# Weights in four tiles, and the first group's output product moved ahead of the third chunk pair

## The chip, the cores and the metric

The kernel runs on one core of a Trainium2 chip. The metric is device time in microseconds (us), the median of several runs. One core has a matrix engine (TensorE; PE in the profile, its weight loads are PEld), a vector engine (VectorE, DVE), a scalar engine (ScalarE, ACT), GpSimd (POOL), and a sync engine (SyncE, SP) that only issues transfers. Each takes its instructions in program order and waits on semaphores. POOL and SP issue nearly all of the DMA transfers; what POOL issues goes through the software queue (q0 in the profile), what SP issues through the hardware queue (q1).

## The reference

Two stages. First a recurrence with decay (a retention layer) over 4 batches, 8 heads, 768 steps and head size 64:

```
gamma = 1.0 - 2.0 ** (-5.0 - np.arange(H))
for t in range(S):
    state = gamma * state + k[:, :, t] (outer) v[:, :, t]
    y[:, :, t] = scale * q[:, :, t] @ state
```

Then, on the 3072 tokens of width 512 that this gives, a feed-forward layer with 2048 hidden units:

```
h = x @ w_in              # (3072, 512) @ (512, 2048)
g = h * np.cos(h)
out = g @ w_out           # (2048, 512)
```

Inputs and output are float32 in memory; the kernel multiplies in bfloat16 and accumulates in float32.

## The kernel before

**Tiles.** Time is cut into six chunks of 128 steps. A *pair* p is one chunk of two batches (b = 0, 1); there are 12 pairs, 0 to 5 for batches 0 and 1, 6 to 11 for batches 2 and 3. Two pairs are one *group* g of 512 tokens, and the feed-forward layer works by groups 0 to 5.

**Attention of one pair.** `load` brings q, k and v, 256 KB per tensor and batch ("q0" is q of batch 0). There are five sets of input buffers (`PRE`), so that pair p takes over the buffers of pair p-5. `conv_q` and `conv_v` scale q and v by powers of gamma and make bfloat16 (on DVE or POOL), `conv_k` only converts (ACT). `stage_t` transposes q and k on TensorE with the identity (L176, 16 per pair) and copies the result to `qkt` (L178 on DVE, L180 on ACT); `stage_t_dma` does the same with two DMA transposes from SP (L186). Pairs below `PT` go through TensorE. `stage_a` computes the scores (L205, 32 matmuls per pair that run two at a time), `stage_m` multiplies them by the causal mask into `am` (L214, four DVE operations per pair). `stage_y` multiplies with the running state (L228) and with v (L233), copies the result to `xt` on ACT (L237), then updates the state (L245) and copies it to `stb` (L250).

**Feed-forward.** `unit_f(g, f)` is one hidden block of 128 units for the 512 tokens of a group: four matmuls of 512 columns (L267), cosine on ACT (L258), product on DVE into `gt` (L262). `pair_f(p, r)` is the same for one pair's 256 tokens and four hidden blocks: 16 matmuls of 256 columns (L279). Its parts (0, 1) are two halves of eight matmuls. `unit_o(g, j, part)` multiplies four hidden blocks of one 128-token tile j with `w_out` (L293, four matmuls of 512 columns, 16 for a whole tile) and, after part 3, copies the bank to `ob` (ACT, L305) and stores it (SP, L306).

**PSUM.** Seven banks of 128x512 float32 are handed out from a first-in first-out list; the eighth holds the state. A matmul that takes a bank waits until the bank's last reader is done.

**Order.** It is written out by hand. After the attention of pairs 0 and 1, group 0's F blocks are computed (`pair_f` of pairs 0 and 1), with the third pair's attention (p = 2) between the last blocks; then group 1's F blocks with pair 3's attention between them; and then a regular loop over g from 1 that alternates `unit_o(g-1, ...)` with `unit_f(g, ...)` and lays one pair's attention into each half of it. Group 0's output product (64 matmuls of L293) thus comes after all of group 1's F.

**Transfers before the loop.** SP: q0, k0, q1 of pair 0; q0, v0 of pair 1; q0, q1 of pair 2; q0, q1, v0 of pair 4; then pairs 5 and 6. POOL:

```
load(nc.gpsimd, 1, ("k0", "q1", "k1", "v1"))
load_w_in(0, 256)
load_w_in(1, 256)
load_w_in(1)
...
load(nc.gpsimd, 3, ("v0", "v1"))
for r in range(4):
    load_w_out(r)
```

`w_in_sb` is one tile whose columns are in the order of memory; a load of 512 columns reads 1 MB of float32 in runs of 2 KB and writes 512 KB of bfloat16. `load_w_out(r)` reads 512 rows of 2 KB each, again 1 MB.

Of the kernel before, what the change touches and what calls it, by code (L numbers as in the profile page):

```python
# [11 lines left out]
BF16 = mybir.dt.bfloat16  # L12
# [18 lines left out]
def kernel(  # L31
# [9 lines left out]
    nc = tc.nc  # L41
# [8 lines left out]
    NP = B // 2 * NC  # L50
    NG = NP // 2
    PRE = 5
    PT = 5

    scale = 1.0 / math.sqrt(D)
    lg = [math.log(1.0 - 2.0 ** (-5.0 - h)) for h in range(H)]
# [7 lines left out]
    def sb(shape, dt, name):  # L64
        return const.tile(shape, dt, name=name)
# [8 lines left out]
    lnsc = sb([128, 1], FP32, "lnsc")  # L74
    sb([128, 1], FP32, "pad")

    w_in_sb = sb([128, KIN, DF], BF16, "w_in_sb")
    w_out_sb = sb([128, KOUT, DM], BF16, "w_out_sb")


# [24 lines left out]
    def load(eng, p, names):  # L105
        bp, c = divmod(p, NC)
        for n in names:
            t, src = SRC[n[0]]
            b = int(n[1])
            eng.dma_start(  # L110
                out=t[p % PRE][b],
                in_=src[2 * bp + b, :, ds(c * C, C)].rearrange("h t d -> t h d"))

    def load_w_in(r, n=512):
        nc.gpsimd.dma_start(
            out=w_in_sb[:, :, ts(r, n)],
            in_=moe_w_in[:, ts(r, n)].rearrange("(i p) f -> p i f", p=128))

    def load_w_out(r):
        nc.gpsimd.dma_start(  # L120
            out=w_out_sb[:, ts(r, 4), :],
            in_=moe_w_out[ts(r, 512), :].rearrange("(f p) m -> p f m", p=128))


    nc.gpsimd.iota(pos, pattern=[[C, NC]], base=1, channel_multiplier=1,
                   allow_small_or_imprecise_dtypes=True)
    load(nc.sync, 0, ("q0", "k0", "q1"))
    load(nc.sync, 1, ("q0", "v0"))
    load(nc.gpsimd, 0, ("k1", "v0", "v1"))
    make_identity(nc, ident)  # L130
    nc.vector.memset(zero, 0.0)
    nc.vector.memset(lnsc, math.log(scale))
# [17 lines left out]
    def conv_q(p, eng):  # L150
        for b in range(2):
            eng.tensor_tensor(out=qs[p % NB][:, b], in0=qf[p % PRE][b],  # L152
                              in1=bc(gq, p % NC), op=ALU.mult)

    def conv_v(p, eng):
        for b in range(2):
            eng.tensor_tensor(out=vs[p % NB][:, b], in0=vf[p % PRE][b],  # L157
                              in1=bc(gk, p % NC), op=ALU.mult)

    def conv_k(p, on_act):  # L160
        for b in range(2):
            if on_act:
                nc.scalar.copy(out=ks[p % NB][:, b], in_=kf[p % PRE][b])  # L163
            else:
                nc.vector.tensor_copy(out=ks[p % NB][:, b], in_=kf[p % PRE][b])
# [24 lines left out]
    def qt(n, b, a):  # L190
        return qkt[n][:, 0, b, a, :]

    def kt(n, b, a):
        return qkt[n][:, 1, b, a, :]

    def stage_a(p):
        n = p % NB
        todo = []
        for b in range(2):
            bk = [banks.take(), banks.take()]  # L200
            ap = [t.rearrange("p (a t) -> p a t", a=HP) for t in bk]
            for a in range(HP):
                for j in range(2):
                    po = 64 * j
                    nc.tensor.matmul(ap[j][:, a, :], lhsT=kt(n, b, a)[po : po + 64, :],  # L205
                                     rhs=qt(n, b, a)[po : po + 64, :],
                                     tile_position=(po, 0))
            todo.append((b, bk, ap))
        return todo

    def stage_m(p, item):
        b, bk, ap = item
# [51 lines left out]
    def unit_f(g, f):  # L264
        bank = banks.take()
        for i in range(KIN):
            nc.tensor.matmul(bank, lhsT=w_in_sb[:, i, ts(f, 128)], rhs=xt[g % 2][:, i, :],  # L267
                             start=(i == 0), stop=(i == KIN - 1))
        act(bank, gt[g % 2][:, f, :])
        banks.give(bank)  # L270

    def pair_f(p, r, parts=(0, 1)):

        g, hf = divmod(p, 2)
        for f in [4 * r + 2 * i for i in parts]:
            bank = banks.take()
            for e in range(2):
                for i in range(KIN):
                    nc.tensor.matmul(bank[:, ts(e, 256)], lhsT=w_in_sb[:, i, ts(f + e, 128)],  # L279
                                     rhs=xt[g % 2][:, i, ts(hf, 256)],  # L280
                                     start=(i == 0 and e == 0), stop=(i == KIN - 1),
                                     skip_group_check=True)
            act(bank, gt[g % 2][:, f : f + 2, ts(hf, 256)])
            banks.give(bank)
# [2 lines left out]

    def unit_o(g, j, part):
        if part == 0:
            o_bank[0] = banks.take()  # L290
        bank = o_bank[0]
        for f in range(4 * part, 4 * part + 4):
            nc.tensor.matmul(bank, lhsT=gt[g % 2][:, f, ts(j, 128)], rhs=w_out_sb[:, f, :],  # L293
                             start=(f == 0), stop=(f == KOUT - 1))
        if part == 3:
            o = ob[j % 4]
            bp, c = divmod(2 * g + j // 2, NC)
            dst = out[ds((2 * bp + j % 2) * S + c * C, C), :]
            if g == NG - 1 and j == 3:
                nc.vector.tensor_copy(out=o[:, ts(0, 256)], in_=bank[:, ts(0, 256)])  # L300
                nc.sync.dma_start(out=dst[:, ts(0, 256)], in_=o[:, ts(0, 256)])
                nc.scalar.copy(out=o[:, ts(1, 256)], in_=bank[:, ts(1, 256)])
                nc.scalar.dma_start(out=dst[:, ts(1, 256)], in_=o[:, ts(1, 256)])
            else:
                nc.scalar.copy(out=o, in_=bank)  # L305
                nc.sync.dma_start(out=dst, in_=o)  # L306
            banks.give(bank)
# [7 lines left out]
            nc.tensor.matmul(spare, lhsT=zero[:, :128], rhs=zero, start=True, stop=True,  # L315
                             skip_group_check=True)

    def masks(p, items):
        for it in items:
            stage_m(p, it)  # L320

    load(nc.gpsimd, 1, ("k0", "q1", "k1", "v1"))
    load_w_in(0, 256)
    load_w_in(1, 256)
    load_w_in(1)
    load(nc.sync, 2, ("q0", "q1"))
    load(nc.sync, 4, ("q0", "q1", "v0"))
    conv_v(1, nc.gpsimd)
    load_w_in(2)
    load(nc.gpsimd, 2, ("k0", "k1"))  # L330
    load_w_in(3)
    load(nc.gpsimd, 2, ("v0", "v1"))
    load(nc.gpsimd, 3, ("k0", "q0", "k1", "q1"))
    conv_q(2, nc.gpsimd)
    conv_v(2, nc.gpsimd)
    load(nc.gpsimd, 3, ("v0", "v1"))
    for r in range(4):
        load_w_out(r)

    warm(10)  # L340
    conv_q(0, nc.vector)
# [1 line left out]
    conv_v(0, nc.vector)  # L343
    stage_t(0, False)
    warm(3)
    m0 = stage_a(0)
    masks(0, m0)
    conv_k(1, True)
    conv_q(1, nc.vector)
    warm(6)  # L350
    stage_y(0, nc.scalar.copy)
    conv_v(3, nc.gpsimd)
    load(nc.gpsimd, 4, ("k0", "k1", "v1"))
    warm(2)
    stage_t(1, None)
    m1 = stage_a(1)
    masks(1, m1)
    pair_f(0, 0)
    banks.give(spare)
    stage_y(1, nc.scalar.copy)  # L360
    pair_f(1, 0)
    for r in (1, 2):
        pair_f(0, r)
        pair_f(1, r)
    conv_k(2, True)
    pair_f(0, 3)
    stage_t(2, None)
    pair_f(1, 3, (0,))
    m2 = stage_a(2)
    masks(2, m2)  # L370
    pair_f(1, 3, (1,))
    stage_y(2, nc.scalar.copy)
    load(nc.sync, 5, ("q0", "q1", "v0"))
    conv_q(4, nc.gpsimd)
    load(nc.gpsimd, 5, ("k0", "k1", "v1"))
    pair_f(2, 0)
    conv_k(3, True)
    conv_q(3, nc.vector)
    pair_f(2, 1)
    stage_t(3, None)  # L380
    pair_f(2, 2, (0,))
    m3 = stage_a(3)
    masks(3, m3)
    pair_f(2, 2, (1,))
    pair_f(2, 3)
    stage_y(3, nc.scalar.copy)
    conv_v(4, nc.gpsimd)
    load(nc.sync, 6, ("q0", "q1", "v0"))
    load(nc.gpsimd, 6, ("k0", "k1", "v1"))
    for r in range(4):  # L390
        pair_f(3, r)
        if r == 2:
            conv_k(4, True)


    todo = []
    for g in range(1, NG + 1):
        for s in range(16):
            hf, r = divmod(s, 8)
            p = 2 * (g + 1) + hf  # L400
            if 1 < g < NG:
                unit_f(g, s)
            unit_o(g - 1, *divmod(s, 4))
            if p < NP:
                if r == 0 and p + 1 < NP:
                    conv_q(p + 1, nc.gpsimd)
                    conv_k(p + 1, True)
                    conv_v(p + 1, nc.gpsimd)
                elif r == 1 and p < PT:
                    stage_t(p, False)  # L410
                elif r == 2:
                    todo = stage_a(p)
                    stage_m(p, todo[0])
                    if PT <= p + 1 < NP:
                        stage_t_dma(p + 1)
                elif r == 3:
                    stage_m(p, todo[1])
                elif r == 6:
                    stage_y(p)
                    if p + 3 < NP:  # L420
                        load(nc.sync, p + 3, ("q0", "q1", "v0"))
                        load(nc.gpsimd, p + 3, ("k0", "k1", "v1"))


# [28 lines left out]
```

## Time and profile before

| | us |
|---|---|
| Median of 4 runs (219.41 to 221.12) | 219.81 |
| The profiled execution: its own time | 221.12 |
| The profiled execution: its span in the trace | 219.4 |
| TensorE busy in that span | 205.6 (94%) |
| DVE / ACT / POOL busy | 115.7 / 116.1 / 85.9 |

The page gives busy times over the whole span. In the 40 slices each digit is the busy share of one fortieth of the span (5.5 us) in tenths, and PEclk is the clock granted to TensorE in tenths of full speed. The regular loop, from about 74 us on, has TensorE busy all the time; what varies lies before that. A matmul's recorded duration includes its way through the array, so neighbouring matmuls overlap in the records (379 ns recorded, one every 216 ns).

### The profile page before, as it was taken

How to read it: one execution, taken by the hardware profiler on the slowest of the kernel's cores; microseconds unless marked ns; L12 is line 12 of the kernel's file. 1: busy time of each engine (PE TensorE's matmuls, PEld its weight loads, DVE VectorE, ACT ScalarE, POOL GpSimd, SP SyncE). 2: the span in 40 equal slices, each digit the busy share in tenths (PEclk: the TensorE clock that was granted, in tenths of full speed). 3: DMA queues.
4: the chain of work that ended last, by engine and by line, in shares of the span. 5: the costliest groups of instructions: out<-in, count | busy, mean ns of one | idle time of the engine just before them, and what ended most of it. 6: DMA issues, size and time to landing. Idle time of an engine off the chain costs nothing.

```text
span 219.4 us, 4276 instructions
## 1 busy us (share of the span) xinstructions
PE 205.6 (94%) x1701; PEld 113.3 (52%) x1701; DVE 115.7 (53%) x185; ACT 116.1 (53%) x185; POOL 85.9 (39%) x98
## 2 busy tenths in 40 slices
PE   7588987789999999999999999999999999999993
PEld 3357875658855454444544544544544544444441
DVE  4397669578744515657557447547647234433000
ACT  7555784817883354484464474564544644444120
POOL 7968379891299991766640420000000000000000
PEclk9799999969999999999999999999999999999999
DMA  6999999999858999999952651051011011110212
GB/s 158 329 242 195 245 304 277 181 196 268 244 151 211 274 229 270 195 252 250 276 168 75 160 139 53 3 143 49 3 48 48 3 48 48 48 50 2 96 63 80
DMA packets 58676, 33.31 MB, mean 152 GB/s; under 512 B 48224, under 2 KB 53088, under 8 KB 58656
## 3 DMA queue, kind: packets, MB, share of 16 engines
q1 hardware_dynamic: 50480, 17.96, 35.3%
q0 software_dynamic: 8032, 14.95, 27.2%
q8 instruction: 13, 0.21, 0.4%
q10 hardware_dynamic: 144, 0.13, 0.2%
q14 instruction: 7, 0.06, 0.1%
HBM read 27.26 MB, written 6.29 MB: 153 GB/s over the span
## 4 chain that ended last, share of the span: by engine, by line
PE 82%; DVE 7%; ACT 5%; DMA 2%; issue 1%; SPq 0%; DVEq 0%; ACTq 0%
PE bank L293 37%; PE bank L267 26%; PE bank L279 10%; PE bank L205 3%; DVE qs L152 2%; DMA qf<-in_q_dram 2%; DVE am L214 2%; PE bank L228 2%; PE bank L233 2%; ACT cosb L258 2%; DVE gt L262 1%; ACT xt L237 1%; PE bank L176 1%; ACT ks L163 1%; ACT qkt L180 1%
## 5 line engine op out<-in xcount | busy, mean ns | idle before, releaser
L262 DVE TENSOR_TENSOR gt<-bank,cosb 128x512 bf16<-128x512 f32 x96 | 65.9, 690 | 69.7 <-ACT cosb L258 69.6
L258 ACT ACTIVATE cosb<-bank,halfpi 128x512 bf16<-128x512 f32 x96 | 65.7, 687 | 64.6 <-PE bank L267 49.9
L293 PE MATMUL bank<-w_out_sb,gt 128*128 128x512 bf16 x384 | 94.3, 379 | 0.0
L267 PE MATMUL bank<-xt,w_in_sb 128*128 128x512 bf16 x256 | 65.8, 379 | 0.0
L293 PEld LDWEIGHTS <-gt 128*128 128x128 bf16 x384 | 37.2, 98 | 44.2
L267 PEld LDWEIGHTS <-w_in_sb 128*128 128x128 bf16 x256 | 24.1, 98 | 28.3
L214 DVE TENSOR_TENSOR am<-bank,mask 128x512 bf16<-128x512 f32 x48 | 30.2, 682 | 5.6 <-PE bank L205 3.1
L279 PE MATMUL bank<-xt,w_in_sb 128*128 128x256 bf16 x256 | 30.3, 277 | 2.0 <-ACT xt L237 1.4
L157 POOL TENSOR_TENSOR vs<-vf,gk 128x512 bf16<-128x512 f32 x22 | 22.9, 1056 | 14.9 <-DMA vf<-in_v_dram 14.7
L279 PEld LDWEIGHTS <-w_in_sb 128*128 128x128 bf16 x256 | 25.0, 99 | 5.7 <-issue 1.5
L152 POOL TENSOR_TENSOR qs<-qf,gq 128x512 bf16<-128x512 f32 x18 | 19.2, 1082 | 21.2 <-DMA qf<-in_q_dram 18.4
L110 POOL DMA_DIRECT2D kf<-in_k_dram x23 | 20.9, 910 | 3.3 <-DMA w_in_sb<-in_moe_w_in_dram 2.9
L305 ACT COPY ob<-bank 128x512 f32<-128x512 f32 x23 | 13.5, 585 | 16.3 <-PE bank L293 16.3
L237 ACT CAST xt<-bank 128x512 bf16<-128x512 f32 x24 | 13.0, 587 | 10.3 <-PE bank L233 10.3
L163 ACT CAST ks<-kf 128x512 bf16<-128x512 f32 x24 | 13.8, 615 | 3.4 <-DMA kf<-in_k_dram 3.4
L110 POOL DMA_DIRECT2D vf<-in_v_dram x15 | 13.3, 891 | 0.0
L233 PE MATMUL bank<-am,vs 128*64 128x128 bf16 x192 | 12.1, 220 | 0.9 <-DVE am L214 0.9
L250 DVE CAST stb<-st_ps 64x512 bf16<-64x512 f32 x12 | 8.3, 689 | 6.5 <-PE st_ps L245 6.3
L228 PEld LDWEIGHTS <-stb 128*64 128x64 bf16 x160 | 8.7, 109 | 4.4 <-issue 4.2
L233 PEld LDWEIGHTS <-vs 128*64 128x64 bf16 x192 | 10.1, 110 | 1.5 <-issue 0.5
L228 PE MATMUL bank<-qkt,stb 128*64 128x128 bf16 x160 | 10.6, 222 | 0.0
L205 PE MATMUL bank<-qkt 64*128 64x128 bf16 x192 | 8.8, 232 | 1.3 <-DVE qkt L178 0.9
(38 smaller groups left out, 75.7 us busy)
## 6 DMA issues: line engine op xcount, KB each, us to landing
kf<-in_k_dram POOLq DMA_DIRECT2D x23, 256.0 KB, 5.5
out_dram<-ob SPq DMA_DIRECT2D x23, 256.0 KB, 2.1
qf<-in_q_dram SPq DMA_DIRECT2D x21, 256.0 KB, 7.6
vf<-in_v_dram POOLq DMA_DIRECT2D x15, 256.0 KB, 6.0
vf<-in_v_dram SPq DMA_DIRECT2D x9, 256.0 KB, 7.9
w_out_sb<-in_moe_w_out_dram POOLq DMA_DIRECT2D x4, 512.0 KB, 13.3
w_in_sb<-in_moe_w_in_dram POOLq DMA_DIRECT2D x3, 512.0 KB, 12.2
qf<-in_q_dram POOLq DMA_DIRECT2D x3, 256.0 KB, 8.3
```

What stands on the lines that cost most here:

```text
L110: eng.dma_start(out=t[p % PRE][b], in_=src[2 * bp + b, :, ds(c * C, C)].rearrange("h t d -> t h d"))
L152: eng.tensor_tensor(out=qs[p % NB][:, b], in0=qf[p % PRE][b], in1=bc(gq, p % NC), op=ALU.mult)
L157: eng.tensor_tensor(out=vs[p % NB][:, b], in0=vf[p % PRE][b], in1=bc(gk, p % NC), op=ALU.mult)
L163: nc.scalar.copy(out=ks[p % NB][:, b], in_=kf[p % PRE][b])
L214: nc.vector.tensor_tensor(out=am[p % 2][b][j], in0=ap[j], in1=mask.unsqueeze(1).to_broadcast([128, HP, 128]), op=ALU.mult)
L228: nc.tensor.matmul(yp[ts(j, 64), a, :], lhsT=stb[p % 2][:, b, a, ts(j, 64)], rhs=qt(n, b, a), start=True, stop=False, skip_group_check=True)
L233: nc.tensor.matmul(yp[ts(j, 64), a, :], lhsT=vs[n][:, b, 2 * a + j, :], rhs=am[p % 2][b][j][:, a, :], start=(c == 0), stop=True, skip_grou ...
L258: nc.scalar.activation(out=cb, in_=bank, func=AF.Sin, bias=halfpi)
L262: nc.vector.tensor_tensor(out=out, in0=bank, in1=cb, op=ALU.mult)
L267: nc.tensor.matmul(bank, lhsT=w_in_sb[:, i, ts(f, 128)], rhs=xt[g % 2][:, i, :], start=(i == 0), stop=(i == KIN - 1))
L279: nc.tensor.matmul(bank[:, ts(e, 256)], lhsT=w_in_sb[:, i, ts(f + e, 128)], rhs=xt[g % 2][:, i, ts(hf, 256)], start=(i == 0 and e == 0), s ...
L293: nc.tensor.matmul(bank, lhsT=gt[g % 2][:, f, ts(j, 128)], rhs=w_out_sb[:, f, :], start=(f == 0), stop=(f == KOUT - 1))
```

## The change

- `w_in_sb` becomes four tiles of 512 hidden units, each loaded whole. `load_w_out` gives each partition four neighbouring rows of `w_out` (8 KB in one run), which puts the hidden units in another order; `w_in_t` picks the matching columns of `w_in`, every fourth one, as the weights of L267 and L279 (L268 and L280 after).
- POOL's transfers are reordered: all of `w_in`, three quarters of `w_out`, q and k of pair 2, the last quarter, v of pair 2, pairs 3 and 4. Pair 2's q moves from SP to POOL. POOL issues k1 of pair 0 ahead of its iota.
- Group 0's blocks 4 to 15 are `unit_f` instead of `pair_f`. Then comes group 0's output product, part by part over four banks at once (`o_bank[j]`), with pair 2's transposes, scores and `stage_y` among its units. Pair 2's conv_q and conv_v move from POOL to DVE, pair 3's conv_q from DVE to POOL.
- Pair 4 is transposed by DMA instead of TensorE (`PT` from 5 to 4). Group 1's output product is split: 8 units before the loop, 8 in the first pass of it, on every second step.
- In pair 1, batch 0's transposed q and k are copied by ACT instead of DVE. `stage_a` is called for one batch at a time.

```diff
-    PT = 5
+    PT = 4
...
-    w_in_sb = sb([128, KIN, DF], BF16, "w_in_sb")
+    w_in_sb = [sb([128, KIN, 512], BF16, f"w_in{r}") for r in range(4)]
...
-            in_=moe_w_out[ts(r, 512), :].rearrange("(f p) m -> p f m", p=128))
+            in_=moe_w_out[ts(r, 512), :].rearrange("(p j) m -> p j m", j=4))
+    def w_in_t(i, f):
+        return w_in_sb[f // 4][:, i].rearrange("p (m j) -> p j m", j=4)[:, f % 4, :]
...
+    load(nc.gpsimd, 0, ("k1",))
     nc.gpsimd.iota(pos, pattern=[[C, NC]], base=1, channel_multiplier=1,
...
-    load(nc.gpsimd, 0, ("k1", "v0", "v1"))
+    load(nc.gpsimd, 0, ("v0", "v1"))
...
-            nc.tensor.matmul(bank, lhsT=w_in_sb[:, i, ts(f, 128)], rhs=xt[g % 2][:, i, :],
+            nc.tensor.matmul(bank, lhsT=w_in_t(i, f), rhs=xt[g % 2][:, i, :],
...
-            o_bank[0] = banks.take()
-        bank = o_bank[0]
+            o_bank[j] = banks.take()
+        bank = o_bank[j]
...
+    def attend(p):
+        for it in [stage_a(p, b) for b in range(2)]:
             stage_m(p, it)
...
-    load_w_in(0, 256)
-    load_w_in(1, 256)
-    load_w_in(1)
-    load(nc.sync, 2, ("q0", "q1"))
-    load(nc.sync, 4, ("q0", "q1", "v0"))
+    for r in range(4):
+        load_w_in(r)
     conv_v(1, nc.gpsimd)
-    load_w_in(2)
-    load(nc.gpsimd, 2, ("k0", "k1"))
-    load_w_in(3)
+    for r in range(3):
+        load_w_out(r)
+    load(nc.gpsimd, 2, ("k0", "q0", "k1", "q1"))
+    load_w_out(3)
     load(nc.gpsimd, 2, ("v0", "v1"))
-    load(nc.gpsimd, 3, ("k0", "q0", "k1", "q1"))
-    conv_q(2, nc.gpsimd)
-    conv_v(2, nc.gpsimd)
-    load(nc.gpsimd, 3, ("v0", "v1"))
-    for r in range(4):
-        load_w_out(r)
+    load(nc.gpsimd, 3, ("k0", "q0", "k1", "q1", "v0", "v1"))
+    load(nc.sync, 4, ("q0", "q1"))
+    load(nc.gpsimd, 4, ("k0", "k1", "v0", "v1"))
...
-    stage_t(1, None)
+    stage_t(1, True)
...
-    for r in (1, 2):
-        pair_f(0, r)
-        pair_f(1, r)
+    for f in range(4, 16):
+        unit_f(0, f)
     conv_k(2, True)
-    pair_f(0, 3)
-    stage_t(2, None)
-    pair_f(1, 3, (0,))
-    m2 = stage_a(2)
-    masks(2, m2)
-    pair_f(1, 3, (1,))
-    stage_y(2, nc.scalar.copy)
+    conv_q(2, nc.vector)
+    for part in range(3):
+        for j in range(4):
+            unit_o(0, j, part)
+            if part == 2 and j == 0:
+                stage_t(2, None)
+    for b in range(2):
+        stage_m(2, stage_a(2, b))
+    conv_v(2, nc.vector)
+    conv_q(3, nc.gpsimd)
     load(nc.sync, 5, ("q0", "q1", "v0"))
+    load(nc.gpsimd, 5, ("k0", "k1", "v1"))
+    conv_v(3, nc.gpsimd)
+    for j in range(4):
+        unit_o(0, j, 3)
+        if j == 2:
+            stage_y(2, nc.scalar.copy)
     conv_q(4, nc.gpsimd)
-    load(nc.gpsimd, 5, ("k0", "k1", "v1"))
+    conv_v(4, nc.gpsimd)
+    conv_k(3, True)
     pair_f(2, 0)
-    conv_k(3, True)
-    conv_q(3, nc.vector)
+    stage_t(3, None)
     pair_f(2, 1)
-    stage_t(3, None)
-    pair_f(2, 2, (0,))
-    m3 = stage_a(3)
-    masks(3, m3)
-    pair_f(2, 2, (1,))
+    attend(3)
+    conv_k(4, True)
+    stage_t_dma(4)
...
+    pair_f(2, 2)
     pair_f(2, 3)
     stage_y(3, nc.scalar.copy)
...
+    attend(4)
+    o_units(1, 0, 4)
+    later(4)
+    attend(5)
+    ahead(6)
+    stage_t_dma(6)
+    o_units(1, 4, 8)
+    later(5)
+    for g in range(2, NG + 1):
         for s in range(16):
...
+            if g == 2 and s % 2 == 0:
+                unit_o(1, *divmod(8 + s // 2, 4))
+            if g < NG:
                 unit_f(g, s)
...
+                elif r == 1:
+                    todo = [stage_a(p, b) for b in range(2)]
+                    stage_m(p, todo[0])
```

In the last lines, `ahead(p)` is conv_q, conv_k and conv_v of a pair, `later(p)` is `stage_y` and the loads of pair p+3, and `o_units(g, a, b)` runs the units a to b-1 of group g's output product in the order tile by tile.

## The prediction

> **What bounds the kernel now.** I read the page first: TensorE's busy share by slice, and the chain that ended last.
>
> ```profile
> PE   7588987789999999999999999999999999999993
> PEclk9799999969999999999999999999999999999999
> DMA  6999999999858999999952651051011011110212
> PE 82%; DVE 7%; ACT 5%; DMA 2%; issue 1%; SPq 0%; DVEq 0%; ACTq 0%
> ```
>
> The chain is TensorE for 82%. From slice 10 (49 us) on its row is nines up to the last; it starves in the first nine slices, and there the DMA row is full. So next the stretches, between landmarks of the PE timeline (start of pair 0's F, of pair 1's F, end of group 0's F, start of group 1's F, of its second half, of group 0's output product):
>
> ```profile
> core 0: us, PE busy (x), PEclk, DMA share, GB/s
> ...
> 21.04:33.20 12.16, 11.53 (x112) 1.00 1.15 270
> 33.20:39.39 6.19, 4.66 (x85) 1.00 1.06 254
> 39.39:53.65 14.26, 11.90 (x144) 0.88 1.19 208
> 53.65:60.64 6.99, 6.99 (x65) 1.00 0.89 252
> 60.64:70.21 9.57, 9.19 (x111) 1.00 0.72 173
> 70.21:219.40 149.19, 145.46 (x1013) 1.00 0.44 115
> ```
>
> After 70.21 only the 3.7 us of the tail are idle: no order of transfers can gain there. Between 21 and 70 us 4.9 are idle, and one stretch has a clock of 0.88. The PE timeline and the windows say why:
>
> ```profile
> 44.09 0.40 PE L176 MATMUL bank<-ident,qs 128*128 128x128 bf16 x4 [1.06 <-DVE qs L152]
> 44.33 0.39 PE L176 MATMUL bank<-ident,ks 128*128 128x128 bf16 x4
> 45.55 0.58 PE L176 MATMUL bank<-ident,qs 128*128 128x128 bf16 x4 [0.83 <-DVE qs L152]
> 45.92 0.63 PE L176 MATMUL bank<-ident,ks 128*128 128x128 bf16 x4
> 46.35 1.91 PE L279 MATMUL bank<-xt,w_in_sb 128*128 128x256 bf16 x8
> ```
>
> ```profile
> 42.20:45.60 3.40, 1.51 (x17) 1.00 1.21 195
> 45.60:49.00 3.40, 3.40 (x32) 0.50 1.22 196
> 35.40:38.80 3.40, 2.83 (x64) 1.00 1.00 244
> ```
>
> Pair 3's transposes wait twice for conv_q on DVE; TensorE is busy 1.51 of 3.4 us, and the next 3.4 us run at clock 0.50 (eight matmuls in 1.91 us, elsewhere one per 0.109 us). A stretch 83% busy had no such sequel. Last, the DMA view of 44 to 50 us, when `w_out` arrives:
>
> ```profile
> q0 software_dynamic: 945, 0.94, 91.7%
> q1 hardware_dynamic: 946, 0.24, 30.0%
> ```
>
> The queues are served packet for packet: 945 software against 946 hardware packets. The software queue moves 1 KB (2 KB read) per turn, the hardware queue 256 B.
>
> **Part by part.** The profiled execution took 221.12 us for a span of 219.4; the median, 219.81, is 0.4 above the span. I sum on the span and subtract from the median.
>
> *The start.* k1 of pair 0 is issued ahead of the iota, which delays the decay table by about 0.9 us (one POOL issue, 882 ns). The first conv_q needs it at 3.92 us, DVE had been idle 0.97 before, and the next waits for q1 (to 7.35); I cost it at nothing, at 0.9 if DVE's slack is not there. In pair 1 one qkt copy moves to ACT, which is free at 15.7 and needs 1.0: ready at 16.7, batch 1 on DVE at 17.0 as before. Pair 0's F starts near 17.4, pair 1's at 21.04, as now.
>
> *Group 0's F.* Pair 1's first block row takes 16 x 0.109 = 1.74 us (64 matmuls in 6.99), then 12 `unit_f` of 4 x 0.2165 (0.866 in the chain) make 10.39: end at 33.2. Is `w_in` there? Quarters landed at 22.2, 25.6 and 30.55 (issue plus time to landing); the last was late because two loads of pair 2 (1.6 us) lay before it, and the first quarter, as two halves, took 4.4 us instead of 3.4. Without both the last lands near 28.0; it is needed at 29.7. The 0.63 us wait goes, with 1.7 to spare (0.7 if halves cost nothing).
>
> *Group 0's output product, parts 0 to 2.* 12 units x 0.866 = 10.39, plus 0.90 for pair 2's transposes (62.36 to 63.26), reached at 41.0. `w_out` quarters now follow `w_in`. Price of one: 3.4 us (the pace of `w_in`) if 8 KB runs change nothing; with runs four times as long the hardware queue gets a quarter of the turns, and I take 3.3. Landings 31.3, 34.6, 37.9; needed at 33.2, 36.6, 40.1. Then four q/k loads of 0.81 (six landed between 30.55 and 35.4): 41.1; I add 0.9, because the last quarter of `w_out` landed 4.9 us after the third, 1.5 more than its pace. q1 at 42.0, conv_q 0.69, batch 1's transposes at 42.7 instead of 41.4: a stall of 1.3. Its bounds are 0.4 (no lag) and 4.6 (`w_in` 1 us later, 3.9 per quarter as in 44.6 to 56.3, 1.16 per load as in 30.55 to 39.8). Queued behind the waiting transposes are three output units, which need nothing from pair 2. Parts 0 to 2 end at 45.8.
>
> *Pair 2's attention.* Scores 2 x 0.28, and between them a wait: with four banks held, three are left, and batch 1 needs one that batch 0's first mask frees (0.69 plus 0.2). 47.2. Three units, 2.6: 49.8. DVE: masks 46.1 to 48.6 (four in 2.48), then conv_v, 1.05 each if POOL converts alongside (two took 2.13 and 2.78 beside POOL, 1.4 alone): 50.7. `stage_y` batch 0 at 49.8, batch 1 at 50.7, state to 51.4, last unit: 52.3. There the F of pair 2 starts. Before, it started at 39.39 with 64 output matmuls still to do, 13.86 us: 53.25. **Gain 0.95** (from 1.9 to a loss of 2.4 with the bounds above).
>
> *Pair 4's transposes*: **0.9 us** off TensorE. The two DMA transposes (3.2 and 2.8 us to landing) are issued by SP behind group 0's four stores; their sources are ready near 58 and the scores come at 70.
>
> *Pairs 3 and 4.* Before, between 39.39 and 70.21: 1.2 and 1.0 us for conv_q, 1.8 at half clock, 0.65 ahead of pair 3's F, 0.5 in pair 4's scores: 5.15 lost. After: conv_q(3) is POOL's and done by 52; conv_k(3) stands on ACT behind the xt, stb and ob copies and ends at 54.6, in time. The cosines behind it end at 55.9, the products at 56.55, the two qkt copies (0.64 each) at 57.2 and 57.85; the scores are reached at 56.7: 0.95 lost. The F of pair 3 waits 0.9 for xt behind the last cosine. In the loop two score sets in a row take four of seven banks; the next F blocks wait perhaps 0.2 each of four times. Together 2.65: **gain 2.5**. No 3.4 us has less than half of TensorE's work, so no half clock; if one comes, 1.7 is lost.
>
> *The weights' new pattern.* The trace has no weight load with a stride. Lower bound: no cost. The nearest rows are contiguous: 128x128 loads of 98 ns recorded, passing one per 56 ns in the transposes. If a load took four times that, 224 ns, it would just fill the 216 ns of a 512-column matmul but exceed the 109 ns of a 256-column one by 115, on the 160 such matmuls left: 18.4 us, and 8 ns on each of 304 others, 2.4 us. I take nothing: the contiguous load has a factor of two to spare even against 109.
>
> The Trainium skill ("TensorE: Matmul & The Clock Gate", Weight-path perf modes) says that the fast weight load reads two bf16 weights at a time; every fourth column would halve that. An estimate from it is 112 ns per load, 0.5 us in all. The trace cannot show it.
>
> *Loads moved to POOL.* Loads that SP issued during `w_in` took 19.8 to 22.4 us to land, those of POOL 10.5 to 13.0: pair 2's q in POOL's queue comes in a known place. The skill ("DMA: Bandwidth & Descriptors", Issuing engine by pattern) sends simple loads to Sync and calls that path generally faster; by it q of pair 2 would come later than 42.0, and these rows say the opposite for a saturated stretch.
>
> Sum: 0.95 + 0.9 + 2.5 = 4.35, less nothing for the start: 219.81 - 4.35, about **215.5 us**.
>
> **Rivals.** *Pair 3 stalls as before* (18%): the products on DVE hold the qkt copies longer and half clock returns. Its 2.5 go: 218.0. For it: ACT carries six copies there. Against: conv_q leaves DVE, whose two took 2.78 us.
>
> *Pair 2 comes too late* (15%): stall 4.6 instead of 1.3, then half clock, 1.7: 220.5. For it: the queue carries 8 MB of weights before q1 is in. Against: packet for packet, and SP has fewer loads.
>
> *The strided loads bind* (13%, the slower side): place, the 160 matmuls of 256 columns. At 136 ns each (27 more) the 4.35 us are gone; at 224 ns the time is 215.5 + 20.8 = 236. For it: nothing in the trace has the pattern. Against: the factor of two.
>
> *It does not do what it says*: the 8 KB runs do not speed the queue. This is inside the forecast, at 0.1 us per quarter.
>
> **Numbers.** The forecast has 50%, the rest 4%. Half a per cent, 1.1 us, is about what a measurement of this kernel can tell from no change. Faster: forecast, pair 3, and a third of pair 2's case, 73%; same 11%; slower 16%, mostly the strided loads. The range runs from 213.2 (stall at its lower bound, no waits in the loop) to 220.0, which leaves out the strided loads and the worst of pair 2.
>
> **What would show it.** Right: group 0's F without a gap to 33.2; the first L294 right behind it; pair 2's transposes waiting at most 2 us for DVE; pair 2's F near 52; clock 1.0 from 12 us on. Wrong: L280 more than 0.12 us apart; L294 waiting for `w_out`; a second window at 0.50.

## The result: 219.33 us against 219.81, and the profile after

The changed kernel takes 219.33 us (median of 53 runs, 217.58 to 223.05); the kernel before, 219.81 us over 79 runs. The ratio of the comparable runs is 0.9952, 95% interval 0.9938 to 0.9967. Ratios here leave out runs more than 1.5% above the fastest of their kernel, which are 15 of the 53 and 7 of the 79, so that this one flatters the change: by the medians of all runs the gain is 0.2%. The forecast was 215.5. Direction right, size wrong: 4.35 us were counted on, and 0.5 arrived by the medians, 1.1 by the ratio.

The profiled execution took 221.27 us for a span of 219.5. It belongs to the longer ones of this kernel. It shows at full size a loss that c0_after, a shorter execution profiled below, has in part; how much of it the median execution has is not shown directly.

The page of the changed kernel: busy tenths, granted clock, DMA share, chain.

```profile
PE   7758999978989994999999999999999999999993
PEclk9999999999999999699999999999999999999998
DMA  6999999999599999999992651051011011110212
PE 81%; DVE 6%; DMA 4%; ACT 3%; POOL 3%; issue 2%; DVEq 0%; POOLq 0%; ACTq 0%
```

The clock of 6 tenths that before had at 44 to 49 us is gone; the PE row still has a 7 there. A new dip, PE at 4 and then a clock of 6 tenths, stands at 82 to 93 us, where both rows of before were nines.

The PE timeline of the changed kernel around the landmarks of the prediction (start, duration, line, shape, count; in brackets the idle time before it and its releaser):

```profile
22.80 10.52 PE L268 MATMUL bank<-xt,w_in 128*128 128x512 bf16 x48
33.16 7.93 PE L294 MATMUL bank<-w_out_sb,gt 128*128 128x512 bf16 x36
40.93 0.39 PE L180 MATMUL bank<-ident,qs 128*128 128x128 bf16 x4
...
45.68 0.38 PE L207 MATMUL bank<-qkt 64*128 64x128 bf16 x7 [0.73 <-DVE am L215]
...
49.63 0.25 PE L234 MATMUL bank<-am,vs 128*64 128x128 bf16 x2 [0.70 <-DVE vs L161]
...
51.08 0.25 PE L234 MATMUL bank<-am,vs 128*64 128x128 bf16 x2 [0.81 <-DVE vs L161]
...
52.72 1.91 PE L280 MATMUL bank<-xt,w_in 128*128 128x256 bf16 x16
...
64.09 7.15 PE L280 MATMUL bank<-xt,w_in 128*128 128x256 bf16 x64 [0.65 <-ACT xt L238]
...
87.44 0.62 PE L207 MATMUL bank<-qkt 64*128 64x128 bf16 x16 [3.00 <-DMA qkt<-ks]
```

Up to 82 us this is nearly the predicted timeline: group 0's F without a gap to 33.2, the output product right behind it, pair 2's transposes reached at 40.9 (41.0 predicted), pair 2's F at 52.7 (52.3), pair 3's at 64.1 (63.8 by the prediction's terms). Then pair 6's score product, L207 at 87.44, waits 3.00 us for its DMA transposes. The windows of the same trace show the sequel:

```profile
core 0: us, PE busy (x), PEclk, DMA share, GB/s
70.70:84.20 13.50, 13.50 (x161) 1.00 1.13 212
84.20:88.40 4.20, 1.20 (x20) 1.00 0.78 181
88.40:91.80 3.40, 3.40 (x9) 0.50 1.02 232
91.80:219.00 127.20, 123.86 (x859) 1.00 0.36 95
```

TensorE is busy for 1.20 of 4.20 us, and the next 3.40 us run at clock 0.50, which costs another 1.70. The prediction had said of everything after 70.21 us that "no order of transfers can gain there". It can lose there, and here lost 3.00 + 1.70 = 4.70 us.

Why the transposes were late is on SP's timeline, changed kernel first:

```profile
76.00 0.36 SPq L307 DMA_DIRECT2D out_dram<-ob  x1
76.45 1.38 SPq L110 DMA_DIRECT2D qf<-in_q_dram  x2
77.93 1.84 SPq L110 DMA_DIRECT2D vf<-in_v_dram  x1
79.94 3.79 SPq L190 DMA_TRANSPOSE qkt<-qs  x1
83.82 1.85 SPq L190 DMA_TRANSPOSE qkt<-ks  x1
```

Then the kernel before, the same two transposes, pair 6's:

```profile
75.39 2.06 SPq L186 DMA_TRANSPOSE qkt<-qs  x1
77.54 3.35 SPq L186 DMA_TRANSPOSE qkt<-ks  x1
```

In both kernels TensorE reaches pair 6's scores at almost the same moment (84.98 before; 87.44 - 3.00 = 84.44 after). But the second transpose, issued at 77.54 before, is issued at 83.82 after: ahead of it now stand a store of group 1 and the three loads of pair 7, which `later(4)` puts into SP's queue before `stage_t_dma(6)`. The scaled q of pair 6 had been ready since 71.1 us (GpSimd ended it there), the converted k since 78.1 (ScalarE).

One number per execution puts all the traces on one scale: when pair 6's scores were reached (start less the wait for their transposes), the wait, and what followed.

| execution | reached, us | wait | half clock after it costs | rest of the span |
|---|---|---|---|---|
| before | 84.98 | 0 | 0 | 134.4 |
| c1_before | 83.17 | 0 | 0 | 134.4 |
| after | 84.44 | 3.00 | 1.7 | 130.4 |
| c0_after | 85.10 | 0.68 | 0 | 130.3 |
| e1_t6_before_loads7 | 85.33 | 0 | 0 | 130.5 |
| e5_qkt1_on_dve | 85.08 | 0 | 0 | 130.4 |
| e10_t6_on_pe_again | 83.16 | 0 | 0 | 130.6 |

The rest is the same within 0.3 us for all kernels with the new order, and 4.0 us shorter than in the kernel before, whose order leaves more for later: six units of output product more and one F block less, in the timelines. So the whole difference between two executions lies in the columns "reached", "wait" and "half clock". "Reached" holds an early loss of its own: in c0_after the clock is at 0.50 from about 7.5 to 14.3 us, in e1_t6_before_loads7 from about 17 to 20.5, and pair 1's F starts at 22.36 and 22.68 there, against 21.05 in the changed kernel's first profile.

### The profile page after: what moved, and what is told of

Read it like the earlier page. It is cut to its first block, busy times and chain, and to the rows that moved or that the text cites. A ratio compares the mean times of both kernels' runs of the same rounds, so it can differ in the third digit from the quotient of the medians.

```text
span 219.5 us, 4150 instructions
## 1 busy us (share of the span) xinstructions
PE 203.5 (93%) x1637; PEld 113.5 (52%) x1637; DVE 116.6 (53%) x186; ACT 114.7 (52%) x184; POOL 83.9 (38%) x98
## 4 chain that ended last, share of the span: by engine, by line
PE 81%; DVE 6%; DMA 4%; ACT 3%; POOL 3%; issue 2%; DVEq 0%; POOLq 0%; ACTq 0%
PE bank L294 37%; PE bank L268 31%; PE bank L280 6%; DMA kf<-in_k_dram 3%; PE bank L207 3%; DVE am L215 2%; PE bank L229 2%; PE bank L234 2%; DVE vs L161 2%; DMA qkt<-ks 2%; ACT xt L238 1%; DVE gt L263 1%; POOL kf L110 1%; PE st_ps L246 1%; POOL vf L110 1%
## 5 line engine op out<-in xcount | busy, mean ns | idle before, releaser
L268 PE MATMUL bank<-xt,w_in 128*128 128x512 bf16 x304 | 76.2, 385 | 0.0
L268 PEld LDWEIGHTS <-w_in 128*128 128x128 bf16 x304 | 34.2, 115 | 32.0 <-issue 2.2
L156 POOL TENSOR_TENSOR qs<-qf,gq 128x512 bf16<-128x512 f32 x18 | 18.5, 1045 | 19.5 <-DMA qf<-in_q_dram 19.3
L161 POOL TENSOR_TENSOR vs<-vf,gk 128x512 bf16<-128x512 f32 x20 | 20.5, 1042 | 6.8 <-DMA vf<-in_v_dram 6.7
L280 PE MATMUL bank<-xt,w_in 128*128 128x256 bf16 x160 | 18.5, 273 | 1.1 <-ACT xt L238 1.1
L280 PEld LDWEIGHTS <-w_in 128*128 128x128 bf16 x160 | 17.3, 113 | 1.5 <-issue 1.0
L110 POOL DMA_DIRECT2D vf<-in_v_dram x16 | 14.2, 888 | 5.1 <-DMA w_out_sb<-in_moe_w_out_dram 5.0
L207 PE MATMUL bank<-qkt 64*128 64x128 bf16 x192 | 8.0, 218 | 6.4 <-DMA qkt<-ks 3.0
L234 PE MATMUL bank<-am,vs 128*64 128x128 bf16 x192 | 11.9, 220 | 2.1 <-DVE vs L161 1.5
L234 PEld LDWEIGHTS <-vs 128*64 128x64 bf16 x192 | 10.1, 110 | 3.5 <-DVE vs L161 1.8
L207 PEld LDWEIGHTS <-qkt 64*128 64x128 bf16 x192 | 5.4, 94 | 11.0 <-issue 4.1
```

The costliest lines, as they stand in the source:

```text
L110: eng.dma_start(out=t[p % PRE][b], in_=src[2 * bp + b, :, ds(c * C, C)].rearrange("h t d -> t h d"))
L234: nc.tensor.matmul(yp[ts(j, 64), a, :], lhsT=vs[n][:, b, 2 * a + j, :], rhs=am[p % 2][b][j][:, a, :], start=(c == 0), stop=True, skip_grou ...
L268: nc.tensor.matmul(bank, lhsT=w_in_t(i, f), rhs=xt[g % 2][:, i, :], start=(i == 0), stop=(i == KIN - 1))
L280: nc.tensor.matmul(bank[:, ts(e, 256)], lhsT=w_in_t(i, f + e), rhs=xt[g % 2][:, i, ts(hf, 256)], start=(i == 0 and e == 0), stop=(i == KIN ...
```

## The experiments

Every one is a short edit of the changed kernel unless it says otherwise. Each was run beside the kernel before on the same chip, and the ratios are to that. c0_after and the runs e1 to e3 share one chip; the others ran elsewhere, so that across these groups the ratios compare, not the medians.

**The changed kernel again, and pair 6's transposes ahead of the loads.**

> The changed kernel again, beside the next three on one chip. Theory T (pair 6's two DMA transposes stand in SP's queue behind pair 7's three loads, come 3 to 4 us late for pair 6's scores, and the idle stretch brings a half clock): a wait of L207 for qkt between 82 and 88 us in the trace, and a ratio near 0.995 to the kernel before. Theory R1 (the weights' pattern costs time everywhere): no such wait in a run that is as slow.

c0_after: 218.28 us (217.84 to 221.48, 6 runs), ratio 0.9898 (0.9854 to 0.9943). Its profile, 217.92 us, has the wait too, but small, and no half clock behind it:

```profile
85.78 0.62 PE L207 MATMUL bank<-qkt 64*128 64x128 bf16 x16 [0.68 <-DMA qkt<-ks]
```

So the loss varies between executions: 4.70 us in one trace, 0.68 in the other.

```
-    later(4)
+    stage_y(4)
+    load(nc.gpsimd, 7, ("k0", "k1", "v1"))
     attend(5)
     ahead(6)
     stage_t_dma(6)
+    load(nc.sync, 7, ("q0", "q1", "v0"))
```

> SP issues pair 7's three loads after pair 6's transposes instead of ahead of them; nothing else moves. T: the wait of L207 near 84 us shrinks from 3.0 to under 1 us (the transposes can start when conv_k(6) ends near 78 and took about 3 us elsewhere), no half clock behind it, and the time falls by 2 to 4 us, to 215.5 to 217.5. R1: no change, 219.3. R2 (transposes are late in any order, since the queues are full): the wait stays above 2 us.

e1_t6_before_loads7: 217.48 us (216.68 to 218.21, 6 runs), ratio 0.9859 (0.9815 to 0.9903). SP's timeline:

```profile
77.48 1.41 SPq L190 DMA_TRANSPOSE qkt<-qs  x1
79.06 1.83 SPq L190 DMA_TRANSPOSE qkt<-ks  x1
80.98 1.16 SPq L110 DMA_DIRECT2D qf<-in_q_dram  x2
```

The second transpose is issued 4.8 us sooner than in the changed kernel's first profile, and the wait is gone: L207 of pair 6 starts at 85.33 with no idle time before it. The median is 0.8 us below that of c0_after on the same chip, and the spread 1.5 us instead of 3.6. The two intervals overlap, so this run alone doesn't settle the size; in its trace the wait goes with the order on SP's queue.

**Pair 6 transposed on TensorE.** `stage_t_dma(6)` is replaced by `stage_t(6, True)` after `o_units(1, 4, 8)`.

> Pair 6 is transposed on TensorE (16 transposes, 0.9 us) between group 1's eighth output unit and stage_y(5), instead of by DMA. T: the wait goes altogether, the time falls by 2 to 4 us less 0.9, to 216 to 218. R1: 220.2, the 0.9 us added. R2: as T.

e2_t6_on_pe: 218.30 us (217.08 to 218.88, 6 runs), ratio 0.9893 (0.9851 to 0.9936). No wait for a DMA transpose either, but the 16 transposes put 0.9 us on TensorE (81.21 to 82.10 in its trace; the 1.7 us for 16 of them in the expectation of e10_t6_on_pe_again below is a misreading). The longest run is 2.6 us shorter than that of c0_after, the median the same: what the transposes cost is about what the wait cost in the median, and near the 0.8 us between c0_after and e1_t6_before_loads7.

**The same lateness put into the kernel before.** If this is the cause, the old order of work must suffer from it as well.

```
-                    if PT <= p + 1 < NP:
+                    if PT <= p + 1 < NP and p != 5:
                         stage_t_dma(p + 1)
...
                         load(nc.gpsimd, p + 3, ("k0", "k1", "v1"))
+                    if p == 5:
+                        stage_t_dma(6)
```

> The kernel before with one thing moved: the DMA transposes of pair 6 are issued after pair 8's loads (step 6 of its half of the loop instead of step 2), four steps or 7 us ahead of pair 6's scores. Theory T (transposes behind three loads in SP's queue come late): a wait of L205 for qkt of 1 to 4 us near 100 us, and 1 to 5 us more than the kernel before, 221 to 225. Rival R2 (the loss of the changed kernel hangs on how full the queues are between 66 and 84 us, not on the order): no wait, 220.

e4_before_late_t6: 227.28 us (223.48 to 230.51, 6 runs), ratio 1.0177 (1.0121 to 1.0232). Its PE timeline, and then its windows:

```profile
89.04 1.04 PE L205 MATMUL bank<-qkt 64*128 64x128 bf16 x16 [4.74 <-DMA qkt<-ks]
```

```profile
84.00:88.16 4.16, 0.30 (x2) 1.00 0.98 160
88.16:94.99 6.83, 5.95 (x28) 0.50 0.93 243
```

The same wait with the same releaser, and here two windows at clock 0.50 behind it. Moving two instructions on SP's queue, with not a matmul changed, makes the kernel before nearly 2% slower by the ratio, and 3% by the medians. This is the clearest of the tests: the cause is the place of these two instructions, not anything that TensorE does.

**The weights' new pattern.** w_in's columns contiguous again, w_out in 2 KB rows:

```
-            in_=moe_w_out[ts(r, 512), :].rearrange("(p j) m -> p j m", j=4))
+            in_=moe_w_out[ts(r, 512), :].rearrange("(f p) m -> p f m", p=128))
...
-        return w_in_sb[f // 4][:, i].rearrange("p (m j) -> p j m", j=4)[:, f % 4, :]
+        return w_in_sb[f // 4][:, i, ts(f % 4, 128)]
```

> The columns of w_in are taken in order and w_out is read in rows of 2 KB, as before the change; the order of all work stays that of the changed kernel. R1: weight loads back to 98 ns and the time falls by 2 us or more. T: the weight loads fall from 113 to 98 ns recorded and nothing is gained by that; w_out comes in 3.4 us per quarter instead of 2.7, so that pair 2's q lands about 2 us later and pair 2's transposes wait about 1 us: 219.5 to 221.

e3_plain_weights: 219.81 us (218.22 to 220.68, 12 runs), ratio 0.9962 (0.9932 to 0.9993); 1.5 us above c0_after on the same chip, the intervals overlapping by a little. The weight-load rows of the page (busy time, mean ns of one), changed kernel first, then this one:

```profile
L268 PEld LDWEIGHTS <-w_in 128*128 128x128 bf16 x304 | 34.2, 115 | 32.0 <-issue 2.2
L280 PEld LDWEIGHTS <-w_in 128*128 128x128 bf16 x160 | 17.3, 113 | 1.5 <-issue 1.0
```

```profile
L268 PEld LDWEIGHTS <-w_in 128*128 128x128 bf16 x304 | 29.1, 98 | 34.5 <-issue 0.2
L280 PEld LDWEIGHTS <-w_in 128*128 128x128 bf16 x160 | 15.4, 98 | 3.3 <-issue 1.1
```

A load of every fourth column is recorded at 113 to 115 ns, a contiguous one at 98. It costs nothing: the 64 matmuls of pair 3's F take 7.15 us with either pattern. The rival "strided loads bind" is out. What this kernel loses instead shows in its trace: it waits 2.42 us at 78.85, for pair 5's transposes already, and a half clock follows. That the slower rows of `w_out` make them late is likely, but not shown.

**The first F, and pair 2's values.** Both start from e1_t6_before_loads7. First `stage_t(1, None)` in place of `stage_t(1, True)`: both copies of pair 1's transposed q and k on VectorE.

> The version with pair 6's transposes first, and both qkt copies of pair 1 on DVE again. The ACT copy ended at 16.8 us, and w_in's first quarter landed at 17.2, 0.2 us ahead of its use: theory T2 (the start is bound by that landing as soon as the copy is out of the way): the scores of pair 1 run 0.7 to 1.3 us sooner, pair 0's F by 0.2 at most: 217.3 to 217.5. Rival: the copy was the bound, and 1 us goes: 216.5.

e5_qkt1_on_dve: 217.25 us (217.06 to 217.75, 6 runs), ratio 0.9864 (0.9834 to 0.9894). The scores of pair 1 start at 16.00 instead of 16.86, and pair 0's F at 17.05. The first quarter of w_in is the next bound: in the profile of e10_t6_on_pe_again, which has this edit too and whose scores start at 15.31, pair 0's F waits 0.82 us for it, to 17.13. The median is 0.2 us lower, on another chip; the ratios, 0.9859 and 0.9864, show no gain.

Then `conv_v(2, nc.gpsimd)` in place of `conv_v(2, nc.vector)`. What it is to cure shows in VectorE's timeline of the changed kernel, and in GpSimd's beside it:

```profile
44.94 2.48 DVE L215 TENSOR_TENSOR am<-bank,mask 128x512 bf16<-128x512 f32 x4 [2.07 <-PE bank L207]
47.34 3.69 DVE L161 TENSOR_TENSOR vs<-vf,gk 128x512 bf16<-128x512 f32 x2
```

```profile
46.97 2.05 POOL L156 TENSOR_TENSOR qs<-qf,gq 128x512 bf16<-128x512 f32 x2
48.96 1.80 POOL L110 DMA_DIRECT2D kf<-in_k_dram  x2
50.75 0.88 POOL L110 DMA_DIRECT2D vf<-in_v_dram  x1
```

> The version with pair 6's transposes first, and pair 2's conv_v on POOL ahead of pair 3's conv_q, instead of on DVE. On DVE the two took 3.0 to 3.7 us beside POOL. Theory T3 (DVE's two-operand float32 work is slowed by POOL's, issues included): POOL makes them in 2.05 us from 47, stage_y(2) waits under 0.3 us instead of 0.8 to 1.5, 0.8 to 1.5 us less, 216.0 to 216.7. Rival: pair 3's conv_q, now 2 us later, becomes late for its transposes at 54.5, and nothing is gained.

e6_v2_on_pool: 218.89 us (215.12 to 221.92, 6 runs), ratio of the comparable ones 0.982 (0.9767 to 0.9874). In its profile the two waits for `vs` are gone and pair 2's F starts at 50.78 instead of 52.72. But the transfers come due sooner as well: pair 5's scores wait 1.22 us for their transposes and pair 6's 3.39, with 6.8 us of half clock around them. Its best runs, 215.12 and 216.30, are near the forecast; its worst, 220.69 and 221.92, are slower than the median of the kernel before.

**All three together, and the queue one pair further up.**

> Pair 6's transposes ahead of pair 7's loads (as in e1_t6_before_loads7), the scores' copy of pair 1 on VectorE (e5_qkt1_on_dve), and the values of pair 2 scaled on GpSimd (e6_v2_on_pool), all together. My theory (the transfers come due as soon as the work in front of them is earlier): pair 2's F starts near 50.5 us, and some of the 2.2 us is lost again in waits for pair 5's or pair 6's DMA transposes of 1 us or more, with a half clock behind them; 216 to 219 us. Rival (the waits in e6_v2_on_pool were chance): no wait for a DMA transpose above 0.3 us, 215 us.

e7_both_sooner: 217.61 us (216.14 to 220.26, 4 runs), ratio 0.9861 (0.977 to 0.9952). Inconclusive: the profiled execution (216.68 us) has no wait for a transpose, but one of the four runs took 220.26.

e8_t5_before_loads6 also moves pair 6's three SP loads behind `stage_t_dma(5)`.

> e7_both_sooner with pair 6's three loads on SP's queue issued behind pair 5's two transposes instead of ahead of them. My theory: pair 5's scores wait under 0.3 us for their transposes, 1 us less than in e6_v2_on_pool; pair 6's loads land later, so pair 6's transposes may be late by 1 us or more instead, with a half clock behind: 215 to 218 us. Rival (the transposes are late because the whole of the DMA engines is full, not because of the order on SP's queue): pair 5's scores still wait 1 us or more, 216 to 219 us.

e8_t5_before_loads6: 217.72 us (214.96 to 221.46, 10 runs), ratio of the comparable ones 0.9794 (0.9746 to 0.9842). Pair 5's wait is gone as expected; pair 6's scores wait 1.12 us and pair 7's 2.55, with a half clock behind the latter. The lateness moves down the chain of pairs.

**A version that beats both.** e9_t6_on_pe is e8_t5_before_loads6 with pair 6 transposed on TensorE (as in e2_t6_on_pe), so that between pair 5's scores (75 us) and pair 7's (96 us) none needs a DMA transpose.

> e8_t5_before_loads6 with pair 6 transposed on TensorE (32 of them, 3.5 us at 0.109 us each) ahead of pair 5's second product, so that no score product waits for a DMA transpose before pair 7. My theory: the half clock of 80 to 93 us is gone in every execution, and the earlier start of 2.4 us stands against 1.7 to 3.5 us more of TensorE: 215 to 217 us, and a smaller spread of the times than e7_both_sooner. Rival (half clocks come from somewhere else): waits of VectorE's or DMA's kind still put a half clock between 40 and 95 us, 217 us or more.

e9_t6_on_pe: 216.78 us (215.56 to 217.63, 4 runs), ratio 0.9831 (0.9774 to 0.9889), and again, in six runs:

> The kernel of e9_t6_on_pe again, in more rounds, on whatever chip this falls on, as the best version so far. (The expectation of e9_t6_on_pe spoke of 32 transposes and 3.5 us; the pair has 16 of them, 1.7 us at 0.109 us.) My theory: 216.8 us again, a ratio of 0.983 to 0.988 and no execution above 218.5 us, since no score product before pair 7 waits for a DMA transpose. Rival (the small spread of e9_t6_on_pe's four runs was chance): some executions at 219 us or more, a median of 217.5 us or more.

e10_t6_on_pe_again: 215.78 us (215.43 to 216.07, 6 runs), ratio 0.9792 (0.9747 to 0.9837). Its page:

```profile
PE   7677999989889999999999999999999999999992
PEclk9999999999999999999999999999999999999998
```

No dip of the clock before the tail, and pair 6's scores start at 83.16 with nothing waited for, although 16 transposes more lie ahead of them. The half clock behind pair 6's scores is gone, and the runs lie within 0.7 us of each other.

The last run of all, the kernel before once more:

> The kernel before, once more in a profile. The first profiled execution took 221.12 us, 1.3 above the median, with one half clock at 45.6 us. Theory T4 (that half clock is not in most runs, so that taking it off the median counted a gain that was not to be had): a run near 219.8 without a half clock between 40 and 60 us. Rival: the half clock is there, and the difference lies outside the span.

c1_before: 219.32 us, span 217.6. Its clock row has no dip:

```profile
PEclk9999999999999999999999999999999999999999
```

The half clock at 45.6 us, from which the prediction took 1.8 us of its gain, belongs to one of the executions profiled: e4_before_late_t6, whose work is the same up to 70 us, doesn't have it either, and six other runs of the kernel before with a mean granted clock of 1.000 took 219.53 to 221.01 us, in the median 219.7. In c1_before the same two waits for conv_q on VectorE are 0.41 and 0.83 us instead of 1.06 and 0.83, the clock stays at 1.00, and pair 3's F starts at 51.84 instead of 53.65. Of these 1.81 us, 0.31 were there before pair 2's F (39.08 instead of 39.39) and 0.65 are the shorter wait. That leaves about 0.85 for the half clock: at full clock two waits for pair 3's copies, 0.30 and 0.20, come up in its place.

## Why the prediction was wrong

*The sum up to 84 us: right against the one execution that it was read from, in part by luck.* It promised 4.35 us on the profiled span. In the table, with the 4.0 us of work that changed its place, the changed kernel reaches pair 6's scores at 84.44 where the kernel before would have been at 84.98 + 4.0 = 88.98: 4.5 us ahead. Against c1_before it is 2.7 ahead. And errors cancel in it: up to pair 2's F the gain is 0.5 (53.25 less 52.72) instead of 0.95, behind it 4.0 instead of 3.4. The steps behind it:

- Group 0's F and w_in: as predicted, no gap to 33.16. Pair 0's F at 17.38, pair 1's at 21.05, as predicted in this execution; in c0_after and e1_t6_before_loads7 the start, costed at nothing, came 1.3 and 1.6 us later, with a half clock ahead of it.
- Pair 2's stall: 1.3 us predicted, 0 measured. The mis-sized terms were w_out's quarter and the lag behind the last one: pair 2's q1, predicted to land at 42.0, was there at 39.6. In e3_plain_weights, with the old rows, it came 1.8 us later, and batch 1's transposes waited for it only 0.1 us. The changed kernel's conv_q first, then that of e3_plain_weights:

```profile
39.62 0.69 DVE L156 TENSOR_TENSOR qs<-qf,gq 128x512 bf16<-128x512 f32 x1 [0.95 <-DMA qf<-in_q_dram]
```

```profile
41.38 0.69 DVE L156 TENSOR_TENSOR qs<-qf,gq 128x512 bf16<-128x512 f32 x1 [0.99 <-DMA qf<-in_q_dram]
```

 The DMA view of the changed kernel from 30 to 42 us:

```profile
q0 software_dynamic: 859, 2.97, 95.1%
q1 hardware_dynamic: 886, 0.22, 10.8%
```

 Still one packet for one packet, but a software packet now carries 3.5 KB on average instead of 1 KB, and the engines move 267 GB/s, against 238 in the same window of e3_plain_weights and 196 in the kernel before from 44 to 50 us. The prediction had these turns in hand and still took 3.3 us where the old price was 3.4; a share by bytes per turn would have given more. That the 8 KB runs do nothing is refuted. "Pair 2 comes too late" did not come true either.
- conv_v(2): 1.05 us each predicted, 2.24 and 1.53 measured (3.69 for two in a row). This is the term that took back the 1.3 of the stall: 0.70 + 0.81 us of waiting in L234. The prediction counted conversions of GpSimd beside it; the second product on VectorE runs beside GpSimd's DMA issues alone and is slow all the same. Why is not shown (last section).
- Pairs 3 and 4: no stall for conv_q and no half clock there, as predicted. The two waits for pair 3's copies are 0.30 and 0.20 (0.95 predicted, where the times given for them make 0.87), the wait for xt 0.65 (0.9).
- The weights' new pattern: nothing, as predicted.

*The step that failed, first: what stands behind a moved step on its queue.* The prediction priced pair 4's two DMA transposes, which the change adds, with their place on SP's queue. It did not do the same for pair 6's, which the change moves behind a store and pair 7's three loads. The rows were there to see, on SP's timeline of the kernel before:

```profile
67.53 0.53 SPq L306 DMA_DIRECT2D out_dram<-ob  x1
68.12 1.43 SPq L110 DMA_DIRECT2D qf<-in_q_dram  x2
69.65 4.21 SPq L110 DMA_DIRECT2D vf<-in_v_dram  x1
```

With the two transposes shown above (2.06 and 3.35) and the 2.8 us that the second of pair 4's took to land, these make 0.53 + 1.43 + 4.21 + 2.06 + 3.35 + 2.8 = 14.4 us (11.4 in the changed kernel's first profile, from 76.00 to 87.44). From the store at 76.0 to the scores at 84.4 there are 8.4. The sentence "no order of transfers can gain there" was read as "none can matter there"; this wait stands in the sum at nothing, and none of the four rivals names it. Size: 0.7 and 4.7 us in the two traces; 0.8 us between the medians of c0_after and e1_t6_before_loads7 on one chip, 1.85 between the median of all 53 runs and e1_t6_before_loads7, with what chips differ by in it.

*The step that failed, second: sum on the span and subtract from the median.* The profiled execution of before stood 1.3 us above the median (221.12 against 219.81), and the gain counted in it included 1.8 us of half clock that c1_before does not have. A gain that consists of removing a mishap can only be claimed as often as the mishap happens. On its own execution the sum would have read 221.12 - 4.35 = 216.8. The half clock was over-priced besides: 1.8 us, where the two traces of the kernel before show about 0.85.

Together: 215.5, plus 1.3 for the mishap, plus 0.7 by which e1_t6_before_loads7 reaches pair 6's scores later than promised (85.33 instead of 88.98 - 4.35 = 84.63; its start is 1.6 us late), is its 217.5. The 0.8 and 1.85 of the late transposes are differences to that run, so that with them the sum meets c0_after and the median by construction, and the second figure can hold more than the transposes.

One bound of the forecast does not follow from its terms: the stall at its lower bound and no waits in the loop take off 0.9 and 0.8, which makes 213.8 and not 213.2.

The rule of the Trainium skill that the prediction weighed ("TensorE: Matmul & The Clock Gate", Weight-path perf modes) bears on the loads of 98 and 113 to 115 ns: a doubling, which the estimate from it took, is not what they show, and the pitch of the matmuls did not change. A rule of the same page (HAM oscillation) warns of idle gaps over about 3.4 us on TensorE; here a gap of 3.00 us in one piece, one of 2.42 in e3_plain_weights, and in the kernel before two waits of 1.06 and 0.83 came before a stretch at 0.50. The idle share does not decide it either. The prediction's "No 3.4 us has less than half of TensorE's work, so no half clock" rested on two rows of the kernel before, and the window of e5_qkt1_on_dve around its waits of 1.73 and 0.81 us for pair 2's values speaks against it:

```profile
48.40:51.80 3.40, 0.86 (x21) 1.00 1.04 357
```

TensorE is busy for 0.86 of 3.40 us, and the clock stays at 1.00 through the window and behind it.

What stays open: why a typical run loses less than the profiled one. In the changed kernel's first profile the issue of pair 6's first transpose holds SP for 3.79 us, in c0_after for 2.02. The second is then issued at 83.82 and at 81.44, and lands 3.6 and 4.3 us later: the difference lies in the issue, not in the landing. In c0_after the scores are also reached 0.7 us later. One thing differs ahead of it: GpSimd, which waited longer for pair 6's q and v, issued its next three loads at 75.2 to 77.9 us in the first profile and at 71.9 to 74.6 in c0_after. Whether these hold up the transposes no run tested.

## What to carry to other kernels

When an edit moves a step up or down, list for every DMA that it issues what now stands before it in its queue and how long before its use it is issued; a chain of work that is "all TensorE" becomes a transfer bound as soon as one of its transfers is issued too late. Price a half clock only as often as executions have it, and less the waits that it hides: profile the kernel before twice, or compare the profiled execution with the median before summing. And work that comes earlier makes its transfers due earlier: in e6_v2_on_pool and e8_t5_before_loads6 another pair's transposes became the next wait, until pair 6's were taken off the queue altogether.

## What was not expected of the hardware

- Two VectorE products of 128x512 took 2.24 and 1.53 us while GpSimd converted for the first 1.7 us and then only issued loads; elsewhere two take 1.4. In c0_after they ran almost wholly beside the issues, and took 1.60 and 1.53. But issues alone do not make it: earlier in the changed kernel's trace, with GpSimd issuing loads from 37.05 to 41.4 us, two products of the same shape took 0.69 each:

```profile
37.97 0.69 DVE L156 TENSOR_TENSOR qs<-qf,gq 128x512 bf16<-128x512 f32 x1 [3.20 <-DMA qf<-in_q_dram]
39.62 0.69 DVE L156 TENSOR_TENSOR qs<-qf,gq 128x512 bf16<-128x512 f32 x1 [0.95 <-DMA qf<-in_q_dram]
```

  The Trainium skill ("SBUF — State Buffer", Who interferes with whom) states that the two engines share one pair of ports under an exclusive lock; no run here isolates that cause, and what tells the two cases apart stays open. With the product moved to GpSimd itself (e6_v2_on_pool, e10_t6_on_pe_again) both waits are gone.
- Bytes per packet go with the share of a saturated stretch: 859 software and 886 hardware packets in 12 us moved 2.97 and 0.22 MB.
- How much idle time brings a half clock has no simple answer here: 1.20 us busy of 4.20, and 1.51 of 3.40, were followed by one; 2.27 of 3.50 (c1_before, 42.0 to 45.5) and 0.86 of 3.40 (e5_qkt1_on_dve, above) were not.
